# Decode attention beside a SwiGLU block on one core: one kv head of all four batches at a time, in runs of 16 to 32 KB

## The chip, the core and the metric

The kernel runs on one core of a Trainium2 chip. The metric is the device time of one execution in microseconds (us), the median of the runs shown. TensorE (PE) multiplies, VectorE (DVE), ScalarE (ACT) and GpSimd (POOL) work on elements, SyncE (SP) issues most of the transfers from the chip's memory (HBM), which 16 DMA engines carry out. A profile shows a single execution.

## The reference

One token for each of four batches goes through a layer norm, an attention over the last 4096 positions of a cache, and a SwiGLU block beside it; both are added to the input.

```python
x = A_x                                   # (4, 1, 512), bf16
xn = _layernorm(x)
# A: attention. 32 query heads, 8 kv heads, head size 128, window W = 4096 of 16384
q = (xn @ wq).reshape(4, 1, 32, 128)      # wq 512 x 4096
k = k_cache[:, :, Sk - W:, :]             # (4, 8, 4096, 128); 4 query heads share a kv head
v = v_cache[:, :, Sk - W:, :]
p = softmax(q @ k^T * 128 ** -0.5)
a = (p @ v).reshape(4, 1, 4096) @ wo      # wo 4096 x 512
# B: SwiGLU
b = (silu(xn @ w_gate) * (xn @ w_up)) @ w_down   # 512 x 1792, 512 x 1792, 1792 x 512
return x + a + b
```

The window of K is 4 x 8 x 4096 x 128 x 2 bytes, 33.55 MB, and that of V as much; the weights are 13.9 MB. Everything is read once: 81.01 MB.

## The kernel before

The attention is cut into 32 pairs of a batch and a kv head. Pair i is batch i % 4 of kv head i // 4. Its K is 1 MB, loaded as 128 partitions of 32 positions each, which makes runs of 8 KB; its V likewise. K and V have four buffers each (`KB`, `VB`, `NSL = 4`).

For each pair TensorE transposes the 32 blocks of K (128 positions x 128) in four sets of eight (`transposes`, L321), VectorE copies each set from PSUM to `KT` (`evac`, L239), TensorE multiplies each transposed block by the four query columns (`scores`, L327), ScalarE takes the exponential with no maximum subtracted (L202), and TensorE sums the probabilities with a matrix of ones (L341) and multiplies them by V (`pv`, L343). VectorE then divides (`norm`, L245 to L249). `pv` of a pair runs after the transposes of the next. Before the transposes of each pair TensorE does two matmuls of 512 columns whose result nobody reads, and before the scores a third (`spin`, L333). TensorE's part of this is a loop over the eight kv heads with the four batches written out; the other engines' instructions are written out in full.

SyncE issues nearly every load, in this order: the first half of W_Q, the input x, the second half of W_Q, K of pair 0, W_gate, W_up, W_down, V of pair 0, then K and V of the pairs in turn, then eight blocks of W_O with runs of 4 KB. A K load from the fifth on waits until the transposes of the pair four before are done (`s_tr`), a V load until the `pv` that used its buffer is done (`s_pv`).

Ahead of the loop stand the layer norm, the query projection (L295), the gate and up projections (L303), the gate on ScalarE and VectorE (L253 to L259) and the down projection (L311). Behind it the heads are reordered by matmuls with selection matrices (`permute`, L349, and `perm_copy`, L264), W_O is multiplied in four strips of 128 columns (`wo`, L357), one copy brings the result to SBUF (L279), and SyncE and ScalarE write two quarters of the output each (L191, L206).

Of the kernel before, what the change touches and what calls it, by code (L numbers as in the profile page):

```python
# [10 lines left out]
def bass_parallel_sum__sliding_block_cached__swiglu_ffn__decode_kernel(  # L11
# [18 lines left out]
    NT = W // 128  # L30
# [3 lines left out]
    NPAIR = B * HKV  # L34
    NSL = 4
    NG = 4
    SCALE = float(Dh) ** -0.5
    EPS = 1e-5

    sb = nc.alloc_sbuf_tensor  # L40
    X = sb("x_sb", [B, D], BF16)
    xc = sb("xc", [B, D], FP32)
    xsq = sb("xsq", [B, D], FP32)
    xn = sb("xn", [B, D], FP32)
    st_sum = sb("st_sum", [B, 1], FP32)
# [5 lines left out]
    WQ = sb("wq_sb", [128, NC, HQ * Dh], BF16)  # L51
    WG = sb("wg_sb", [128, NC, F], BF16)
    WU = sb("wu_sb", [128, NC, F], BF16)
    WD = sb("wd_sb", [128, NF, D], BF16)
    WO = sb("wo_sb", [128, HKV, REP, D], BF16)
    QT = sb("qT", [128, HKV, B, REP], BF16)
    QC = sb("qC", [128, B, REP], BF16)
    KB = [sb("kbuf%d" % s, [128, NT, Dh], BF16) for s in range(NSL)]
    VB = [sb("vbuf%d" % s, [128, NT, Dh], BF16) for s in range(NSL)]
    KT = [sb("kT%d" % s, [128, NT, 128], BF16) for s in range(2)]  # L60
    P = [sb("p%d" % s, [128, NT, REP], BF16) for s in range(2)]
    den = sb("den", [128, REP], FP32)
    OT = sb("oT", [128, HKV, REP, B], BF16)
    OP = sb("oP", [128, REP, HKV, B], BF16)
# [4 lines left out]
    sel = sb("sel", [128, REP, REP, 32], BF16)  # L69
    ones = sb("ones", [128, 128], BF16)  # L70
    I4 = sb("i4", [B, B], FP32)
    y0 = sb("y0", [B, D], FP32)
    I4w = sb("i4w", [B, 32], FP32)
    y = sb("y_sb", [128, 128], BF16)

    ps = nc.alloc_psum_tensor
    ps_kt = [ps("ps_kt%d" % s, [128, 512], FP32) for s in range(4)]
    ps_S = ps("ps_s", [128, 512], FP32)
    ps_O = ps("ps_o", [128, 512], FP32)
    ps_m = ps("ps_m", [128, 512], FP32)  # L80
    ps_acc = ps("ps_acc", [128, 512], FP32)

    kt_ps = [t[:].bitcast(BF16).rearrange("p (a b) -> p a b", b=128) for t in ps_kt]
    O_ps = ps_O[:, 0:REP]
    den_ps = ps_O[:, 128:128 + NT * REP]
    gate_ps = ps_m[:, 0:NF * B]
    up_ps = ps_m[:, 64:64 + NF * B]
    perm_ps = ps_m[:].rearrange("p (e k h b) -> p h e k b", e=REP, k=HKV, h=REP)
    q_ps = ps_acc[:, 0:HQ * B]
    down_ps = ps_acc[0:B, :]  # L90
    xT_ps = ps_m[:, 128:128 + NC * B]
# [4 lines left out]
    d_wq = [sem("d_wq%d" % h) for h in range(2)]  # L96
# [4 lines left out]
    d_wo = [sem("d_wo%d" % q) for q in range(HKV)]  # L101
    d_k = [sem("d_k%d" % s) for s in range(NSL)]
    d_v = [sem("d_v%d" % s) for s in range(NSL)]
# [11 lines left out]
    s_ev = sem("s_ev")  # L115
    s_sc = sem("s_sc")
    s_p = sem("s_p")
# [5 lines left out]
    s_dn = sem("s_dn")  # L123
    s_y0 = sem("s_y0")
    s_y = sem("s_y")

    x_ap = A_x.rearrange("b s d -> (b s) d")
    out_ap = out.rearrange("b s (n c) -> n (b s) c", n=NC)
# [4 lines left out]
    wo_ap = A_wo.rearrange("(k p e) n -> k p e n", k=HKV, e=REP)  # L133

    def kv_ap(cache, i):
        return cache[i % B, i // B, Sk - W:, :].rearrange("(p t) d -> p t d", t=NT)

    with nc.Block() as block:

        @block.gpsimd  # L140
        def _(eng):
            eng.memset(ident[:], 0.0)
            eng.memset(I4[:], 0.0)
            eng.memset(I4w[:], 0.0)
            eng.memset(ones[:], 1.0)
            eng.drain()
            eng.affine_select(I4[:], I4[:], pattern=[[-1, B]], compare_op=ALU.not_equal,
                              fill=1.0, base=0, channel_multiplier=1)
            eng.affine_select(ident[:], ident[:], pattern=[[-1, 128]], compare_op=ALU.not_equal,
                              fill=1.0, base=0, channel_multiplier=1)  # L150
            eng.drain()
            eng.tensor_copy(I4w[:, 0:B], I4[:])
            for e in range(REP):
                for h in range(REP):
                    eng.tensor_copy(sel[:, e, h, :], ident[:].rearrange("p (m e) -> p e m", e=REP)[:, e, :])
            eng.memset(P[1][:], 0.0)
            eng.memset(VB[NSL - 1][:], 0.0).then_inc(s_const, 1)

        @block.sync
        def _(eng):  # L160
            def load_k(i):
                if i >= NSL:
                    eng.wait_ge(s_tr, NG * (i - NSL + 1))
                eng.dma_start(KB[i % NSL][:], kv_ap(A_k_cache, i)).then_inc(d_k[i % NSL], 16)  # L164

            def load_v(i):
                if i == NSL - 1:
                    eng.wait_ge(s_pv, 1)
                if i >= NSL:
                    eng.wait_ge(s_pv, i - NSL + 2)  # L170
                eng.dma_start(VB[i % NSL][:], kv_ap(A_v_cache, i)).then_inc(d_v[i % NSL], 16)  # L171

            def load_wo(q):
                eng.dma_start(WO[:, q], wo_ap[q]).then_inc(d_wo[q], 16)  # L174

            eng.dma_start(WQ[:, 0:2], wq_ap[:, 0:2]).then_inc(d_wq[0], 16)
            eng.dma_start(X[:], x_ap).then_inc(d_x, 16)
            eng.dma_start(WQ[:, 2:4], wq_ap[:, 2:4]).then_inc(d_wq[1], 16)
            load_k(0)
# [3 lines left out]
            load_v(0)  # L183
            for i in range(1, NPAIR):
                load_k(i)
                load_v(i)
            for q in range(HKV):
                load_wo(q)
            eng.wait_ge(s_y, 1)
            for n in range(0, NC, 2):  # L190
                eng.dma_start(out_ap[n], y[32 * n:32 * n + B, :]).then_inc(d_out, 16)  # L191
            eng.wait_ge(d_out, 16 * NC)

        @block.scalar
        def _(eng):
            eng.wait_ge(s_var, 1)
# [3 lines left out]
            for j in range(NPAIR):  # L200
                eng.wait_ge(s_sc, j + 1)
                eng.activation(P[j % 2][:], ps_S[:, 0:NT * REP].rearrange("p (t h) -> p t h", h=REP),  # L202
                               ACT.Exp, scale=SCALE).then_inc(s_p, 1)
            eng.wait_ge(s_y, 1)
            for n in range(1, NC, 2):
                eng.dma_start(out_ap[n], y[32 * n:32 * n + B, :]).then_inc(d_out, 16)  # L206

        @block.vector
        def _(eng):
# [15 lines left out]
            eng.tensor_scalar(xn[:], xc[:], st_rstd[:, 0:1], None, ALU.mult).then_inc(s_xn, 1)  # L225
            eng.wait_ge(s_xT, 1)
            eng.tensor_copy(XnT[:], xT_ps.rearrange("p (c b) -> p c b", b=B)).then_inc(s_xnT, 1)
            eng.wait_ge(s_q, 1)
            eng.tensor_copy(QT[:], q_ps.rearrange("p (k h b) -> p k b h", k=HKV, b=B))
            eng.drain()  # L230
            eng.tensor_copy(QC[:], QT[:, 0]).then_inc(s_nrm, 1)

            eng.engine_nop().then_inc(s_ev, 3)

            def evac(i):
                for g in range(NG * i, NG * i + NG):
                    eng.wait_ge(s_tr, g + 1)
                    a = 8 * (g % NG)
                    eng.tensor_copy(KT[i % 2][:, a:a + 8, :], kt_ps[g % 4]).then_inc(s_ev, 1)  # L239

            def norm(j):
                eng.wait_ge(s_pv, j + 2)
                if j + B < NPAIR:
                    eng.tensor_copy(QC[:, j % B], QT[:, j // B + 1, j % B])  # L244
                eng.tensor_reduce(den[:], den_ps.rearrange("p (t h) -> p h t", h=REP), AX.X, ALU.add)  # L245
                eng.drain()
                eng.reciprocal(den[:], den[:])  # L247
                eng.drain()
                eng.tensor_tensor(OT[:, j // B, :, j % B], O_ps, den[:], ALU.mult).then_inc(s_nrm, 1)  # L249

            def ffn():
                eng.wait_ge(s_ex, 1)
                eng.tensor_scalar(ex[:], ex[:], 1.0, None, ALU.add)  # L253
                eng.drain()
                eng.reciprocal(ex[:], ex[:])
                eng.drain()
                eng.tensor_tensor(gs[:], gate_ps.rearrange("p (t b) -> p t b", b=B), ex[:], ALU.mult)
                eng.drain()
                eng.tensor_tensor(guT[:], up_ps.rearrange("p (t b) -> p t b", b=B), gs[:], ALU.mult).then_inc(s_guT, 1)  # L259

            def perm_copy(n, a, b):
                eng.wait_ge(s_pm, n)
                for h in range(REP):
                    last = eng.tensor_copy(OP[32 * h:32 * h + 32, :, a:b], perm_ps[32 * h:32 * h + 32, h, :, a:b])  # L264
                last.then_inc(s_pc, 1)

            ffn()
            for i in range(NPAIR):
# [4 lines left out]
                if i > 0:  # L273
                    norm(i - 1)
# [138 lines left out]
```

## Time and profile before

| | |
|---|---|
| median of 3 runs | 202.87 us (202.86 to 202.94) |
| span of the profiled execution | 201.0 us |
| TensorE busy | 167.7 us (83%) |
| VectorE busy | 108.7 us (54%) |
| ScalarE, GpSimd busy | 11.9 us, 7.2 us |
| main DMA queue | 81.01 MB, 97.2% of 16 engines' span |
| mean granted TensorE clock | 0.934 |

The span goes from the first to the last instruction of the profiled execution; the measured time lies 1.9 us above it. A line of a group in the profile gives the source line, the engine, the operation, output and inputs by name, shapes and count, then the busy time in us and the mean duration of one in ns, and behind the second bar the idle time of the engine ahead of it. A line of the timeline gives start and length in us. A line of a window gives its bounds, its length, the busy time and count of PE, PEld, DVE, ACT and POOL, the granted clock (PEclk), the busy share of the DMA engines and GB/s.

### The profile page before, as it was taken

Reading aid. Unit: us, or ns where it says so; the run is one execution under the profiler, and the core shown is the slowest. Engines: PE = TensorE matmul, PEld = TensorE weight load, DVE = VectorE, ACT = ScalarE, POOL = GpSimd, SP = SyncE. Lnnn points to the kernel's source line nnn. Section 1 sums busy time; section 2 is a strip of 40 time slices with the busy share of each in tenths; the row PEclk is TensorE's granted clock in tenths of the full one; section 3 lists DMA queues with packets and bytes.
Section 4 is the critical chain, followed back from the end, with each engine's and each line's share of the span. In section 5 each row is a group of like instructions: output and inputs, shape, how many; then the busy total and the mean of one; then the engine's idle time right before and its main releaser. Section 6 shows DMA issues by size and latency. Waiting matters only on the chain.

```text
span 201.0 us, 8038 instructions
## 1 busy us (share of the span) xinstructions
PE 167.7 (83%) x3635; PEld 142.7 (71%) x3635; DVE 108.7 (54%) x277; ACT 11.9 (6%) x36; POOL 7.2 (4%) x29
## 2 busy tenths in 40 slices
PE   0043778999899999999999999988898999898982
PEld 0043662788798888788877987777777987796961
DVE  0330010666666777766666666666665676565740
ACT  2020000010000000001000000000000000000000
POOL 8600000000000000000000000000000000000000
PEclk9999999999969999999999799999998899878755
DMA  6999999999999999999999999999999999999980
GB/s 232 428 425 426 431 418 414 421 417 424 422 411 419 422 422 426 422 419 419 424 422 424 422 416 421 422 424 422 422 419 421 424 424 422 421 419 412 410 334 7
DMA packets 11138, 81.15 MB, mean 404 GB/s; under 512 B 1268, under 2 KB 1272, under 8 KB 2296
## 3 DMA queue, kind: packets, MB, share of 16 engines
q1 hardware_dynamic: 11112, 81.01, 97.2%
q8 instruction: 6, 0.10, 0.2%
q14 instruction: 4, 0.03, 0.0%
q10 hardware_dynamic: 16, 0.00, 0.0%
HBM read 81.01 MB, written 0.00 MB: 403 GB/s over the span
## 4 chain that ended last, share of the span: by engine, by line
DMA 52%; PE 27%; DVE 13%; SPq 5%; issue 2%; ACT 0%; DVEq 0%
DMA kbuf<-in_A_k_cache_dram 32%; DVE kT L239 12%; DMA wu_sb<-in_B_w_up_dram 11%; PE ps_kt L321 10%; DMA wo_sb<-in_A_wo_dram 9%; PE ps_s L327 6%; SPq L174 3%; PE ps_m L333 3%; PE ps_o L343 3%; PE ps_acc L311 3%; PE ps_m L303 2%; SPq L171 1%; PE ps_o L341 0%; PE ps_acc L357 0%; SPq L164 0%
## 5 line engine op out<-in xcount | busy, mean ns | idle before, releaser
L239 DVE COPY kT<-ps_kt 128x1024 bf16<-128x1024 bf16 x128 | 80.9, 684 | 51.9 <-PE ps_kt L321 51.8
L321 PEld LDWEIGHTS ps_kt<-ident,kbuf 128*128 128x128 bf16 x1024 | 65.3, 104 | 15.1 <-issue 7.9
L321 PE MATMUL ps_kt<-ident,kbuf 128*128 128x128 bf16 x1024 | 69.4, 231 | 4.3 <-DMA kbuf<-in_A_k_cache_dram 4.2
L327 PEld LDWEIGHTS ps_s<-qC,kT 128*128 128x128 bf16 x1024 | 28.2, 96 | 12.5 <-DVE kT L239 12.0
L327 PE MATMUL ps_s<-qC,kT 128*128 128x4 bf16 x1024 | 30.4, 164 | 4.2 <-DVE kT L239 4.2
L343 PE MATMUL ps_o<-p,vbuf 128*128 128x4 bf16 x1056 | 31.5, 165 | 0.0
L343 PEld LDWEIGHTS ps_o<-p,vbuf 128*128 128x128 bf16 x1056 | 30.4, 96 | 0.8 <-issue 0.8
L333 PE MATMUL ps_m<-wq_sb,ones 128*128 128x512 bf16 x96 | 31.0, 377 | 0.0
L202 ACT ACTIVATE p<-ps_s 128x128 bf16<-128x128 f32 x32 | 8.9, 277 | 152.5 <-PE ps_s L327 152.5
L287 PE MATMUL ps_m<-i,xn 4*128 4x4 f32 x4 | 0.6, 254 | 12.3 <-DVE xn L225 12.3
L245 DVE TENSOR_REDUCE den<-ps_o 128x4 f32<-128x128 f32 x32 | 9.0, 283 | 0.6 <-PE ps_o L343 0.4
L287 PEld LDWEIGHTS ps_m<-i,xn 4*128 4x128 f32 x4 | 0.6, 208 | 12.3 <-issue 12.3
L341 PE MATMUL ps_o<-p,ones 128*128 128x128 bf16 x33 | 7.5, 228 | 0.7 <-issue 0.7
L333 PEld LDWEIGHTS ps_m<-wq_sb,ones 128*128 128x128 bf16 x96 | 7.0, 96 | 0.4 <-issue 0.4
L303 PE MATMUL ps_m<-xnT,wg_sb 128*128 128x4 bf16 x56 | 3.5, 199 | 4.4 <-DMA wg_sb<-in_B_w_gate_dram 4.4
L247 DVE RECIPROCAL den<-den 128x4 f32<-128x4 f32 x32 | 5.7, 178 | 2.7 <-issue 0.4
L249 DVE TENSOR_TENSOR oT<-ps_o,den 128x4 bf16<-128x4 f32 x32 | 5.4, 168 | 2.7 <-issue 0.4
L253 DVE TENSOR_SCALAR ex<-ex 128x56 f32<-128x56 f32 x1 | 0.2, 192 | 12.0 <-ACT ex L199 12.0
L303 PEld LDWEIGHTS ps_m<-xnT,wg_sb 128*128 128x128 bf16 x56 | 3.4, 159 | 4.5 <-DMA wg_sb<-in_B_w_gate_dram 4.5
L311 PE MATMUL ps_acc<-wd_sb,guT 128*4 128x512 bf16 x14 | 5.1, 542 | 1.7 <-DVE guT L259 1.7
L357 PE MATMUL ps_acc<-wo_sb,oP 128*4 128x128 bf16 x128 | 4.3, 305 | 1.7 <-DMA wo_sb<-in_A_wo_dram 1.7
L244 DVE COPY qC<-qT 128x4 bf16<-128x4 bf16 x28 | 4.4, 158 | 1.2 <-PE ps_o L343 1.0
(46 smaller groups left out, 41.8 us busy)
## 6 DMA issues: line engine op xcount, KB each, us to landing
kbuf<-in_A_k_cache_dram SPq DMA_DIRECT2D x32, 1024.0 KB, 15.5
vbuf<-in_A_v_cache_dram SPq DMA_DIRECT2D x32, 1024.0 KB, 13.7
wq_sb<-in_A_wq_dram SPq DMA_DIRECT2D x2, 2048.0 KB, 9.4
wo_sb<-in_A_wo_dram SPq DMA_DIRECT2D x8, 512.0 KB, 18.4
wg_sb<-in_B_w_gate_dram SPq DMA_DIRECT2D x1, 1792.0 KB, 18.5
wu_sb<-in_B_w_up_dram SPq DMA_DIRECT2D x1, 1792.0 KB, 22.3
wd_sb<-in_B_w_down_dram SPq DMA_DIRECT2D x1, 1792.0 KB, 26.1
out_dram<-y_sb SPq DMA_DIRECT2D x2, 1.0 KB
```

Source lines behind the costliest of these rows:

```text
L174: eng.dma_start(WO[:, q], wo_ap[q]).then_inc(d_wo[q], 16)
L202: eng.activation(P[j % 2][:], ps_S[:, 0:NT * REP].rearrange("p (t h) -> p t h", h=REP), ACT.Exp, scale=SCALE).then_inc(s_p, 1)
L239: eng.tensor_copy(KT[i % 2][:, a:a + 8, :], kt_ps[g % 4]).then_inc(s_ev, 1)
L245: eng.tensor_reduce(den[:], den_ps.rearrange("p (t h) -> p h t", h=REP), AX.X, ALU.add)
L247: eng.reciprocal(den[:], den[:])
L303: last = mm(o[:, t * B:(t + 1) * B], w[:].rearrange("p c (m t) -> p c t m", t=NF)[:, c, t, :], XnT[:, c, :], start=(w is WG and t == 0 and ...
L311: last = mm(down_ps, guT[:, t, :], WD[:, t, :], start=(t == 0), stop=(t == NF - 1))
L321: last = eng.transpose(kt_ps[n % 4][:, k, :], KB[b][:, 8 * g + k, :], ident[:])
L327: last = mm(ps_S[:, REP * t:REP * (t + 1)], KT[b % 2][:, t, :], QC[:, b])
L333: mm(ps_m[:], ones[:], WQ[:, 0, 0:512])
L341: mm(den_ps, ones[:], P[p % 2][:].rearrange("p t h -> p (t h)"))
L343: last = mm(O_ps, VB[p][:, t, :], P[p % 2][:, t, :], start=(t == 0), stop=(t == NT - 1))
```

## The change

The unit of work becomes a group: one kv head of all four batches. Partition p holds batch p % 4 and 128 positions, so K of a group is 4 MB in two halves of 16 KB runs, and V 4 MB in one load of 32 KB runs. K has one buffer, made of the two halves, and V one buffer.

A block of K now holds 32 positions of each of the four batches. Its transposed form is multiplied by all 16 query columns of the kv head; of the 16 scores in a row only the four of the row's own batch are meant. A new step takes the maximum of every column over its batch and adds, by one matmul per PSUM bank (`shift`), the negative maximum to the meant scores and -1e9 to the others, so that their exponential is zero. P therefore holds 16 columns per block, and `pv` sums over all four batches at once.

ScalarE takes over four of the 16 copies of transposed sets in a group (`ACT_CH`). TensorE, VectorE and ScalarE run loops over the groups; TensorE's loop has nine passes with branches, and a pass works on the K of group r and the V of group r - 1. The spins are gone. The three buffers `ps_kt` replace four.

SyncE's order of loads is new: W_Q as one load, W_gate, W_up, both halves of K of group 0, ten of the 32 rows per partition of W_O, then for each further group the two halves of its K and the V of the group before, then the last V, W_down, twenty rows and two rows of W_O. The input x is loaded by ScalarE. The down projection moves from ahead of the loop to behind it; the heads are reordered by four matmuls and one copy; W_O is multiplied in two strips of 256 columns; VectorE and ScalarE bring half of the result each to SBUF, and SyncE and ScalarE write one half each.

```diff
-    NSL = 4
-    NG = 4
+    NJ = 128 // B
+    NT = W // NJ
+    NH = B * REP
+    CH = 8
+    NCH = NT // CH
+    NB = 4
+    BT = NT // NB
+    ACT_CH = (2, 6, 10, 14)
+    WOA = 10
+    WOB = 30
...
-    KB = [sb("kbuf%d" % s, [128, NT, Dh], BF16) for s in range(NSL)]
-    VB = [sb("vbuf%d" % s, [128, NT, Dh], BF16) for s in range(NSL)]
+    KB = sb("kbuf", [128, NT, Dh], BF16, 512)
+    VB = sb("vbuf", [128, NT, Dh], BF16, 512)
...
+    def kv_ap(cache, g, a, b):
+        return cache[:, g, Sk - W:, :].rearrange("b (j t) d -> j b t d", j=NJ)[:, :, a:b, :]
...
+            def load_k(g, h):
+                if g > 0:
+                    eng.wait_ge(s_tr, NCH * (g - 1) + (h + 1) * NCH // 2)
+                eng.dma_start(KB[:, h * H:(h + 1) * H, :], kv_ap(A_k_cache, g, h * H, (h + 1) * H)).then_inc(d_k[h], 16)
+
+            def load_v(g):
+                if g > 0:
+                    eng.wait_ge(s_pv, g + 1)
+                eng.dma_start(VB[:], kv_ap(A_v_cache, g, 0, NT)).then_inc(d_v, 16)
...
+            eng.dma_start(WQ[:], wq_ap).then_inc(d_wq, 16)
+            eng.dma_start(WG[:], wg_ap).then_inc(d_wg, 16)
             eng.dma_start(WU[:], wu_ap).then_inc(d_wu, 16)
+            load_k(0, 0)
+            load_k(0, 1)
+            load_wo(0, 0, WOA)
+            for g in range(1, HKV):
+                load_k(g, 0)
+                load_k(g, 1)
+                load_v(g - 1)
+            load_v(HKV - 1)
             eng.dma_start(WD[:], wd_ap).then_inc(d_wd, 16)
+            load_wo(1, WOA, WOB)
+            load_wo(2, WOB, NR)
...
+            with eng.Fori(0, HKV) as r:
+                for n, c in enumerate(ACT_CH):
+                    eng.wait_ge(s_tr, r * NCH + (c + 1))
+                    eng.activation(KT[:, c % 4], kt_ps[c % 3], ACT.Copy).then_inc(s_ea, 1)
+                eng.wait_ge(s_pv, r + 1)
+                for q in range(NB):
+                    eng.wait_ge(s_mk, r * NB + (q + 1))
+                    eng.activation(P[:, BT * q:BT * (q + 1), :], ps_S[q][:].rearrange("p (t n) -> p t n", n=NH),
+                                   ACT.Exp, scale=SCALE).then_inc(s_p, 1)
...
+            def maxima(r):
+                eng.wait_ge(s_m, r + 1)
+                eng.transpose(mT_ps, m16[:], ident[:]).then_inc(s_mt, 1)
+
+            def shift(r):
+                eng.wait_ge(s_cm, r + 1)
+                for q in range(NB):
+                    mm(ps_S[q][:].rearrange("p (t n) -> p t n", n=NH), own[:],
+                       CM[:].unsqueeze(1).to_broadcast([NH, BT, NH]),
+                       start=False, stop=True, skip_group_check=True).then_inc(s_mk, 1)
+
+            def pv(r):
+                eng.wait_ge(d_v, r * 16)
+                for t in range(NT):
+                    last = mm(O_ps, VB[:, t, :], P[:, t, :], start=(t == 0), stop=(t == NT - 1), skip_group_check=True)
+                last.then_inc(s_pv, 1)
+
+            with eng.Fori(0, HKV + 1) as r:
+                with eng.If(r < HKV):
+                    for c in range(NCH):
+                        transposes(r, c)
+                        if c >= 2:
+                            scores(r, c - 2)
+                    scores(r, NCH - 2)
+                    scores(r, NCH - 1)
+                with eng.If(r > 0):
+                    denominators(r)
+                with eng.If(r < HKV):
+                    maxima(r)
+                with eng.If(r > 0):
+                    pv(r)
+                with eng.If(r < HKV):
+                    shift(r)
...
-            def spin(n):
-                for _ in range(n):
-                    mm(ps_m[:], ones[:], WQ[:, 0, 0:512])
...
+            for t in range(NF):
+                for n in range(2):
+                    mm(acc_ps[64 * n:64 * n + B, 0:H], guT[:, t, :], WD[:, t, H * n:H * (n + 1)],
+                       start=False, stop=False, skip_group_check=True)
+            eng.wait_ge(s_nrm, HKV + 1)
...
+            for q in range(3):
                 eng.wait_ge(d_wo[q], 16)
+                a, b = ((0, WOA), (WOA, WOB), (WOB, NR))[q]
+                for e in range(a, b):
+                    for n in range(2):
+                        last = mm(acc_ps[64 * n:64 * n + B, 0:H], OP[:, e, :], WO[:, e, H * n:H * (n + 1)],
+                                  start=False, stop=(e == NR - 1), skip_group_check=True)
```

More of the change, by code (lines that the diff above doesn't have):

```diff
@@ L50, in bass_parallel_sum__sliding_block_cached__swiglu_ffn__decode_kernel @@
     XnT = sb("xnT", [128, NC, B], BF16)
[L51 to L57, printed above, removed]
-    KB = [sb("kbuf%d" % s, [128, NT, Dh], BF16) for s in range(NSL)]
-    VB = [sb("vbuf%d" % s, [128, NT, Dh], BF16) for s in range(NSL)]
[L60 to L64, printed above, removed]
+    QT = sb("qT", [128, HKV, NH], BF16)
+    QC = sb("qC", [128, NH], BF16)
+    mx = sb("mx", [128, NB, NH], FP32)
+    m16 = sb("m16", [128, NH], BF16)
+    junk = sb("junk", [NH, 128], FP32)
+    M = sb("m", [NH, 1], FP32)
+    CM = sb("cm", [NH, NH], BF16)
+    den = sb("den", [128, NH], FP32)
+    on = sb("on", [128, NH], FP32)
+    OT = sb("oT", [128, B, HKV, REP, 4], BF16)
+    OP = sb("oP", [128, NR, B], BF16)
     ex = sb("ex", [128, NF, B], FP32)
@@ L95, in bass_parallel_sum__sliding_block_cached__swiglu_ffn__decode_kernel @@
     d_x = sem("d_x")
[L96 removed]
+    d_wq = sem("d_wq")
     d_wg = sem("d_wg")
@@ L153, in _ @@
[L153 to L157, printed above, removed]
+            eng.memset(own[:], 1.0)
+            eng.memset(moff[:], 0.0)
+            eng.memset(coff[:], 0.0)
+            eng.memset(neg[:], 0.0)
+            eng.memset(dq[:], 1.0)
+            eng.memset(dr[:], 0.0)
@@ L235, in evac @@
[L235 to L245, printed above, removed]
+            eng.reciprocal(ex[:], ex[:])
@@ L246, in norm @@
+            def norm(r):
+                eng.wait_ge(s_pv, r + 2)
+                eng.tensor_reduce(den[:], den_ps.rearrange("p (t n) -> p n t", n=NH), AX.X, ALU.add)
                 eng.drain()
@@ L309, in _ @@
+            H = D // 2
             eng.wait_ge(d_wd, 16)
+            for n in range(2):
+                mm(acc_ps[64 * n:64 * n + B, 0:H], I4[:], xf[:, H * n:H * (n + 1)],
+                   start=True, stop=False, skip_group_check=True)
             for t in range(NF):
[L311 to L322 removed]
@@ L362, in _ @@
-            eng.wait_ge(s_nrm, 1)
-            with eng.Fori(0, HKV) as r:
-                for b in range(B):
-                    spin(2)
-                    transposes(r, b)
-                    pv(r, b)
-                    spin(1)
-                    scores(r, b)
-            eng.wait_ge(s_y0, 1)
-            permute(0, HKV - 1)
-            for n in range(NC):
-                mm(ps_acc[32 * n:32 * n + 32, 0:128], I4w[:], y0[:, 128 * n:128 * n + 128],
-                   start=True, stop=False, skip_group_check=True)
```

301 lines of the change are left out of this document (155 added, 146 removed).

## The prediction, made before the changed kernel ran

> **What bounds the kernel now.** I read the page's slices first, then the rate in four windows of the trace, then the start and the end of the timeline.
>
> ```profile
> PEclk9999999999969999999999799999998899878755
> DMA  6999999999999999999999999999999999999980
> GB/s 232 428 425 426 431 418 414 421 417 424 422 411 419 422 422 426 422 419 419 424 422 424 422 416 421 422 424 422 422 419 421 424 424 422 421 419 412 410 334 7
> q1 hardware_dynamic: 11112, 81.01, 97.2%
> ```
>
> The DMA engines are full from the second slice to the 38th. The queue is the bound, and the same 81.01 MB must pass it after the change. So the change is worth what it does to three things: the rate, the moments when the queue stands empty, and what is left to do after the last landing.
>
> ```profile
> 9.00:12.00 3.00, 0.00 (x0) 0.00 (x0) 2.41 (x6) 0.74 (x2) 0.00 (x0) 1.00 1.01 431
> 40.00:170.00 130.00, 122.52 (x2730) 105.66 (x2728) 84.99 (x217) 7.77 (x28) 0.00 (x0) 0.96 1.01 421
> 188.00:194.00 6.00, 5.65 (x178) 4.98 (x180) 4.29 (x16) 0.28 (x1) 0.00 (x0) 0.78 1.02 408
> 194.00:198.00 4.00, 2.28 (x80) 1.45 (x72) 0.00 (x0) 0.00 (x0) 0.00 (x0) 0.50 0.29 114
> ```
>
> The last column is GB/s. The first three windows carry 16 KB runs (W_Q), 8 KB runs (K and V) and 4 KB runs (W_O): longer runs, higher rate. In the last window the 16 rings run dry one after the other.
>
> **The change, part by part.**
>
> *The runs.* At 421 GB/s an 8 KB packet holds one of 16 rings for 16 x 8192 B / 421 GB/s = 0.311 us; at 408 a 4 KB packet holds it for 0.161. A straight line through both gives 0.613 for 16 KB (428 GB/s; its window says 431) and 1.216 for 32 KB (431). K (33.55 MB in 16 KB runs) then takes 78.4 us instead of 79.7, V (as much, in 32 KB runs) 77.8 instead of 79.7, W_O in runs of mostly 10 and 20 KB 9.8 instead of 10.3: **3.7 us less**, and 9.80 + 9.73 = 19.5 us for a group. The ends are no gain, if the runs are cut, and about 6 us, if the longest lie above the line by as much as the first window does.
>
> *The start.* SyncE now queues W_Q, W_gate, W_up, both halves of the first group's K and ten rows of W_O. Next comes K of the second group, which must wait until the first half of group 0 is transposed, since K has one buffer.
>
> ```profile
> 25.50 3.52 PE L303 MATMUL ps_m<-xnT,wu_sb 128*128 128x4 bf16 x56 [0.78 <-DMA wu_sb<-in_B_w_up_dram]
> 30.71 5.09 PE L311 MATMUL ps_acc<-wd_sb,guT 128*4 128x512 bf16 x14 [1.69 <-DVE guT L259]
> 34.09 0.13 PEld L311 LDWEIGHTS ps_acc<-wd_sb,guT 128*4 128x4 bf16 x1 [0.30 <-issue]
> 34.51 0.78 PEld L311 LDWEIGHTS ps_acc<-wd_sb,guT 128*4 128x4 bf16 x4 [0.30 <-issue]
> L176 SPq DMA_DIRECT2D wq_sb<-in_A_wq_dram x1: 401/401/401, 0.7 to 0.7; - x1
> DMA to landing us min/median/max: 7.4/7.4/7.4
> ```
>
> W_up was waited for until 25.5. The 1.05 MB of K ahead of it (2.5 us) is gone, and W_Q's runs are longer: 22.9 now. With its 3.52 us of matmuls and 1.69 us for the gate, TensorE enters its loop at 28.1. The halves of K land at 27.8 and 32.7, the W_O rows (1.31 MB) at 35.8. A DMA into empty rings landed 7.4 us after its issue, though its 2.1 MB take 4.9: starting a dry queue costs 2.5.
>
> ```profile
> L239 DVE COPY kT<-ps_kt 128x1024 bf16<-128x1024 bf16 x128 | 80.9, 684 | 51.9 <-PE ps_kt L321 51.8
> L219 DVE TENSOR_REDUCE st_sum<-xsq 4x1 f32<-4x512 f32 x1 | 0.7, 673 | 0.1
> L245 DVE TENSOR_REDUCE den<-ps_o 128x4 f32<-128x128 f32 x32 | 9.0, 283 | 0.6 <-PE ps_o L343 0.4
> L321 PE MATMUL ps_kt<-ident,kbuf 128*128 128x128 bf16 x1024 | 69.4, 231 | 4.3 <-DMA kbuf<-in_A_k_cache_dram 4.2
> L343 PE MATMUL ps_o<-p,vbuf 128*128 128x4 bf16 x1056 | 31.5, 165 | 0.0
> L333 PE MATMUL ps_m<-wq_sb,ones 128*128 128x512 bf16 x96 | 31.0, 377 | 0.0
> L202 ACT ACTIVATE p<-ps_s 128x128 bf16<-128x128 f32 x32 | 8.9, 277 | 152.5 <-PE ps_s L327 152.5
> 99.83 1.95 PE L321 MATMUL ps_kt<-ident,kbuf 128*128 128x128 bf16 x32
> 101.67 0.95 PE L343 MATMUL ps_o<-p,vbuf 128*128 128x4 bf16 x32
> 185.11 3.42 PE L321 MATMUL ps_kt<-ident,kbuf 128*128 128x128 bf16 x32 [0.76 <-DMA kbuf<-in_A_k_cache_dram]
> ```
>
> Less one matmul's length, 32 transposes start every (1.95 - 0.23)/31 = 0.056 us at the full clock and every 0.103 at half; small matmuls every (0.95 - 0.17)/31 = 0.025. The sixteen-column scores and sums aren't in this trace: between 0.025 and a transpose's 0.056, taken at 0.025, because the weights are loaded as before and 16 columns are nearer to 4 than to 128. A block (8 transposes, 8 score matmuls) costs TensorE 0.65 us warm and 1.03 cold. Of 16 blocks VectorE copies 12 at 0.684 and takes 4 maxima over 512 values, between 0.28 and four times that; at the 0.673 of the 512-value row it needs 0.68 a block. I take 0.70 as the warm pace.
>
> The loop begins cold, as L311 did: the weight loads of L311 come 0.43 apart up to 34.5, 3.8 us after its start. With 5.1 us of half clock, the eighth block is transposed 7.0 us after the entry, at 35.1. K of group 1 is issued then and its half lands at 35.2 + 7.4 = 42.6; without the wait it would be 40.7: **1.9 lost**. Its second half waits for the sixteenth block (8 x 0.70 later, 40.7) and lands at 48.2, **0.7** behind. V of group 0 waits for nothing and lands at 57.9. From above: a cold clock for 6.8 us adds 0.6; from below: none lost, if W_up lands 2 us earlier and the clock warms at once.
>
> *The groups.* TensorE needs 16 x 0.70 plus two blocks of lead (12.6), 8 denominator matmuls of 256 columns (0.9), the sums, 128 x 0.025 + 0.2 = 3.4, and four shift matmuls of 512 columns (0.9): 17.8 of 19.5 us. The spins (96 matmuls in 31.0 us) are gone, so the clock will fall in some groups, for 3.4 us as here (PEclk is the third last column, transposes alone are counted):
>
> ```profile
> 106.29:109.70 3.41, 0.47 (x9) 0.30 (x7) 1.00 1.02 423
> 109.70:113.11 3.41, 3.10 (x31) 2.83 (x27) 0.50 1.02 423
> 113.11:116.53 3.42, 1.51 (x28) 1.61 (x29) 1.00 1.01 422
> ```
>
> A drop costs (0.103 - 0.056) x 31 = 1.5, so 19.3 at most: covered. V lands last in a group, 14.7 after the first half of K, the sums end at 18.1, and the next V has to be queued only by about 23: 5 us of lead. Under this cover lie the chain of the maximum, the doubled work on masked columns, ScalarE's four copies of 1024 values (0.28 to 2.2 us each by the 128-value row, which leaves ScalarE below 13 us) and the registers of the loops. If the cover were gone, each us above 19.5 would count eight times, less the 5. GpSimd's constants and the input row lie under W_Q's 10 us. So V of group 6 lands at 57.9 + 6 x 19.53 = 175.1.
>
> *The last V.* SyncE's order is K7, K7, V6, V7, W_down, W_O, W_O. V has one buffer, so V7 waits until V6 is multiplied. By then all K is in, and the W_down and W_O loads, whose buffers are free, stand behind that wait. V6 lands, 3.5 us of sums follow, V7 is issued at 178.7 and lands 2.5 + 9.7 later at 190.9. Without the wait: 184.8. **6.1 lost**; with sums that cost nothing it would still be 2.5.
>
> *The end.*
>
> ```profile
> 193.00 1.88 PE L357 MATMUL ps_acc<-wo_sb,oP 128*4 128x128 bf16 x64
> 197.79 0.60 PE L357 MATMUL ps_acc<-wo_sb,oP 128*4 128x128 bf16 x16 [0.74 <-DMA wo_sb<-in_A_wo_dram]
> 198.44 0.29 DVE L279 CAST y_sb<-ps_acc 128x128 bf16<-128x128 f32 x1 [4.61 <-PE ps_acc L357]
> 198.76 0.63 SPq L191 DMA_DIRECT2D out_dram<-y_sb  x2
> ```
>
> Now 0.6 us of matmuls follow the last landing. After the change W_down lands at 195.2, twenty rows of W_O at 201.3, the last two at 202.0. Four output strips ran together here (64 matmuls of 128 columns in 1.88, 0.105 for four at half clock); two strips of 256 columns then take 0.21 cold, 0.11 warm. After V7 TensorE is done with the sums at 194.4 and VectorE's normalization at 195.7. W_down's 14 pairs and the input's take 3.4 cold (198.6), reordering the heads 0.7, the first ten W_O rows 2.1 (201.4), twenty rows 4.2 cold or 2.2 warm, two rows 0.4 or 0.2. With 0.3 for the last result this is 206.3 cold, 204.1 warm; after six busy us I take 204.7. So **2.7 us** of matmuls follow the last landing, and the copy and the output DMA take 2.4 (198.4 to 201.0 was 2.6, with two DMAs on each queue). The span is 207.1. The measured 202.87 stands 1.9 above this execution's span of 201.0: **209.0**.
>
> **The rivals.**
>
> *TensorE stays cold without the spins.* The Trainium skill (TensorE: Matmul & The Clock Gate, Part 4: PE-mode transpose) says that transposes do not count as work for the clock gate. By that rule most of the loop's work would not count. The window above speaks against it: 3.10 of its 3.41 us were transposes, and the clock was back at 1.00 in the next. If it happened: 18 x 1.03 + 1.8 + 3.6 + 1.8 = 25.7 a group, 8 x 6.2 - 5 more, 254 us. Chance 0.03.
>
> *The four batches collide in memory.* Four runs of one DMA now lie 33.55 MB apart instead of 8 KB. Rings that move together read different tokens of one batch, as before, so I expect nothing; no row here shows such a distance. At half the rate K and V would take 156 us more, 365. The Trainium skill (DMA: Bandwidth & Descriptors, the row on HBM row pitch at large powers of two) tells of copies that fall to half at pitches of megabytes; no run here shows it. Chance 0.03.
>
> *TensorE's groups are longer than 19.5.* If a sixteen-column matmul costs a transpose's 0.056, the scores and sums add 256 x 0.031 = 7.9, so 25.7 a group, 254 again; if only half of that, 21.8, and 8 x 2.3 - 5 = 13 more: 222. Chance 0.07.
>
> *The long runs are cut.* Then 3.7 is not gained: 212.7. Chance 0.05.
>
> *Not slower.* The losses stand as summed, but the long runs go further above the line. It decides from 6.1 us: K and V in 150.1 instead of 156.2, 447 GB/s; 202.9. For it, the rate rises at each step of 408, 421, 431; against it, by ever less per doubled run. Chance 0.08.
>
> **How the numbers follow.** My forecast, 209.0, has 0.74. Its range: from below, no loss at the start (2.6) and a warm end (0.6) with 2.0 from long runs that lie above the line, 203.8; from above, no gain of runs (3.7) and a cold end (1.6), 214.3. That leaves out part of the last rival and the three slow cases, less than 2 in 10. Faster than 202.87 by over 0.2% (0.4 us, about what this measurement can tell): most of the last rival, 0.06; within it 0.02; slower 0.92.
>
> **What would show it right or wrong.** Right: K and V windows near 428 to 431 GB/s; two dips in the slices, one near 36 us and one of about 6 us near 176; V7's wait for the sums among the queue's waits; W_O matmuls for some 3 us after the last landing; PEclk falling in most groups while DMA stays full. Wrong: TensorE never waiting for K or V in the middle, a flat GB/s row, or a rate of 440 and more.

## The result, and the profile after

The changed kernel takes 208.6 us (median of 4 runs, 208.08 to 210.42), the kernel before 202.89 beside it: a ratio of 1.0295, interval 1.0251 to 1.0339. Five more runs later gave 208.88 and 1.0298 (1.0281 to 1.0315). The forecast was 209.0. The profiled execution has a span of 206.4 and a time of 208.08.

The slices of the changed kernel's page, 5.16 us each, its main queue, its queue of instructions, and the engines' shares of the chain that ended last:

```profile
PEclk9999999966996699699759975997999599855569
DMA  7989995999999999999999999999999995289991
GB/s 249 464 371 428 433 420 238 356 403 454 411 441 457 394 413 416 486 413 413 416 486 413 413 422 480 413 416 429 470 391 435 451 451 248 51 381 426 438 393 43
q1 hardware_dynamic: 4472, 81.01, 92.4%
q8 instruction: 6, 0.10, 0.2%
...
PE 63%; DMA 25%; DVE 5%; ACT 4%; issue 2%; SPq 1%; DVEq 0%
```

The same bytes now take 92.4% of the span in place of 97.2%. The DMA row has two holes, slice 7 (the rate is still low in slice 8) and slices 34 and 35. The windows of the trace measure them:

```profile
34.00:36.40 2.40, 2.40 (x65) 2.40 (x62) 2.39 (x5) 1.02 (x1) 0.00 (x0) 1.00 0.07 24
60.00:172.00 112.00, 109.75 (x2334) 98.89 (x2333) 74.50 (x147) 35.92 (x47) 0.00 (x0) 0.85 1.01 432
172.00:176.00 4.00, 3.63 (x77) 2.94 (x75) 3.08 (x7) 1.02 (x1) 0.00 (x0) 1.00 0.36 156
176.00:180.00 4.00, 3.98 (x117) 3.03 (x113) 1.19 (x5) 0.81 (x2) 0.00 (x0) 0.94 0.00 0
```

Between the holes the queue is faster than before, 432 GB/s against 421: for the 67.1 MB of K and V 155.3 us in place of 159.4. Then from about 174 to 180 almost nothing moves, while TensorE works nearly without a pause on what it has. Who makes the queue wait stands in the waits of SyncE's queue (us in total, times, longest), and who waits for V in those of TensorE:

```profile
SPq L210 <- PE ps_kt L370: 111.3, 14, 30.4
SPq L215 <- PE ps_o L410: 51.3, 7, 19.1
```

```profile
PE ps_o L410 <- DMA vbuf<-in_A_v_cache_dram: 8.3, 2, 8.1
```

Most of SyncE's waiting is harmless, since earlier loads are still under way. It costs only where nothing is left in the rings: at K of group 1, and at V7. TensorE waits for V twice in eight groups, and 8.1 of the 8.3 us are V7. The timeline of the end:

```profile
175.45 3.39 PE L410 MATMUL ps_o<-p,vbuf 128*128 128x16 bf16 x128
178.87 0.54 SPq L215 DMA_DIRECT2D vbuf<-in_A_v_cache_dram  x1
191.28 3.58 PE L410 MATMUL ps_o<-p,vbuf 128*128 128x16 bf16 x128 [8.08 <-DMA vbuf<-in_A_v_cache_dram]
194.90 0.42 DVE L316 TENSOR_REDUCE den<-ps_o 128x16 f32<-128x256 f32 x1 [14.62 <-PE ps_o L410]
195.52 1.02 PE L433 MATMUL ps_kt<-xf,i 4*4 4x256 f32 x4 [0.66 <-DMA wd_sb<-in_B_w_down_dram]
196.47 3.15 PE L437 MATMUL ps_kt<-wd_sb,guT 128*4 128x256 bf16 x28
200.38 3.77 PE L449 MATMUL ps_kt<-wo_sb,oP 128*4 128x256 bf16 x64 [0.53 <-DVE oP L332]
201.58 2.27 PEld L449 LDWEIGHTS ps_kt<-wo_sb,oP 128*4 128x4 bf16 x44 [0.24 <-DMA wo_sb<-in_A_wo_dram]
204.19 0.41 DVE L334 CAST y_sb<-ps_kt 4x256 bf16<-4x256 f32 x1 [3.87 <-PE ps_kt L449]
```

V7 is issued the moment V6's sums are done and lands 12.4 us later. From the end of V7's sums to the copy of y another 9.3 us pass (194.90 to 204.19), in which TensorE waits 0.66 us for W_down and its weight loads (PEld) 0.24 us for W_O.

### The profile page after: what moved, and what is told of

It reads as the page before. It is cut to its first block, busy times and chain, and to the rows that moved or that the text cites. A ratio compares the mean times of both kernels' runs of the same rounds, so it can differ in the third digit from the quotient of the medians.

```text
span 206.4 us, 7990 instructions
## 1 busy us (share of the span) xinstructions
PE 169.8 (82%) x3520; PEld 150.4 (73%) x3520; DVE 109.2 (53%) x217; ACT 52.6 (25%) x69; POOL 7.5 (4%) x29
## 3 DMA queue, kind: packets, MB, share of 16 engines
q1 hardware_dynamic: 4472, 81.01, 92.4%
## 4 chain that ended last, share of the span: by engine, by line
PE 63%; DMA 25%; DVE 5%; ACT 4%; issue 2%; SPq 1%; DVEq 0%
PE ps_kt L370 30%; PE ps_o L410 12%; DMA wu_sb<-in_B_w_up_dram 10%; PE ps_s L383 10%; DMA wd_sb<-in_B_w_down_dram 8%; DMA vbuf<-in_A_v_cache_dram 7%; PE ps_s L403 5%; ACT kT L248 4%; DVE mx L304 2%; PE ps_kt L449 2%; PE ps_s L356 2%; PE ps_kt L437 1%; DVE m L306 1%; PE ps_kt L398 1%; PE ps_kt L433 0%
## 5 line engine op out<-in xcount | busy, mean ns | idle before, releaser
L370 PE MATMUL ps_kt<-ident,kbuf 128*128 128x128 bf16 x1024 | 89.3, 243 | 2.1 <-DVE guT L290 2.1
L299 DVE COPY kT<-ps_kt 128x1024 bf16<-128x1024 bf16 x96 | 64.4, 691 | 21.4 <-PE ps_kt L370 21.2
L248 ACT ACTIVATE kT<-ps_kt 128x1024 bf16<-128x1024 bf16 x32 | 32.7, 1023 | 58.8 <-PE ps_kt L370 58.8
L383 PE MATMUL ps_s<-qC,kT 128*128 128x16 bf16 x1024 | 45.2, 171 | 2.3 <-ACT kT L248 2.3
L383 PEld LDWEIGHTS ps_s<-qC,kT 128*128 128x128 bf16 x1024 | 39.6, 98 | 3.4 <-ACT kT L248 3.0
L410 PE MATMUL ps_o<-p,vbuf 128*128 128x16 bf16 x1024 | 27.4, 170 | 8.3 <-DMA vbuf<-in_A_v_cache_dram 8.3
L252 ACT ACTIVATE p<-ps_s 128x512 bf16<-128x512 f32 x32 | 16.5, 603 | 46.6 <-PE ps_s L403 46.6
L304 DVE TENSOR_REDUCE mx<-ps_s 128x16 f32<-128x512 f32 x32 | 21.9, 683 | 3.6 <-PE ps_s L383 3.6
L403 PE MATMUL ps_s<-cm,own 16*128 16x512 bf16 x32 | 12.7, 536 | 2.2 <-issue 2.2
L393 PE MATMUL ps_o<-p,ones 128*128 128x256 bf16 x64 | 9.1, 290 | 1.4 <-ACT p L252 1.3
```

Of the source, the lines that this page charges most:

```text
L248: eng.activation(KT[:, c % 4], kt_ps[c % 3], ACT.Copy).then_inc(s_ea, 1)
L252: eng.activation(P[:, BT * q:BT * (q + 1), :], ps_S[q][:].rearrange("p (t n) -> p t n", n=NH), ACT.Exp, scale=SCALE).then_inc(s_p, 1)
L299: eng.tensor_copy(KT[:, c % 4], kt_ps[c % 3]).then_inc(s_ev, 1)
L304: eng.tensor_reduce(mx[:, q, :], ps_S[q][:].rearrange("p (t n) -> p n t", n=NH), AX.X, ALU.max)
L370: last = eng.transpose(kt_ps[c % 3][:, k, :], KB[:, CH * c + k, :], ident[:])
L383: last = mm(ps_S[q][:, NH * t:NH * (t + 1)], KT[:, c % 4, k, :], QC[:], start=(t == 0), stop=False, skip_group_check=True)
```

## The experiments

### The last V without its wait

W_Q's buffer has the size of one V and is free after the query projection. V7 goes there, waits only for that, and TensorE's last pass is written out behind the loop.

```diff
-            load_v(HKV - 1)
+            eng.wait_ge(s_q, 1)
+            eng.dma_start(WQF, kv_ap(A_v_cache, HKV - 1, 0, NT)).then_inc(d_v7, 16)
```

> V of the last group goes into W_Q's place, which is free after the query projection, and waits for nothing but that; the last pass of TensorE's loop is written out behind the loop. All else is the changed kernel (span 206.4, 208.6 us). By the sum of the prediction the queue loses 6.1 us on that wait: V7 should land near 185 instead of 191.2, everything behind it 6.1 earlier, span 200.3, time 202.5. Rival: TensorE's own passes set the end, because it is behind the queue (its chain runs from 45 to 141 us without a DMA in it); then V7 lands early, the sums of the last group still start only when TensorE is through, and less than 3 us are gained: 205.6 or more.

Measured: 202.46 us (12 runs, 201.53 to 205.41), ratio to before 0.9972 (0.9954 to 0.9991). Its windows, and its end:

```profile
33.70:36.50 2.80, 2.80 (x68) 2.80 (x67) 2.42 (x5) 1.02 (x1) 0.00 (x0) 1.00 0.09 31
172.00:176.00 4.00, 3.54 (x72) 3.04 (x69) 3.35 (x6) 1.02 (x1) 0.00 (x0) 1.00 0.99 426
176.00:180.00 4.00, 4.00 (x132) 3.61 (x133) 1.20 (x4) 0.16 (x1) 0.00 (x0) 1.00 0.93 401
```

```profile
189.15 0.42 DVE L319 TENSOR_REDUCE den<-ps_o 128x16 f32<-128x256 f32 x1 [8.21 <-PE ps_o L414]
198.64 0.41 DVE L337 CAST y_sb<-ps_kt 4x256 bf16<-4x256 f32 x1 [4.11 <-PE ps_kt L455]
```

Where 156 and 0 GB/s stood, 426 and 401 stand; the first hole is still there. 208.6 - 202.46 is 6.1 us, the price that the prediction put on this wait; in the two profiled executions the copy of y comes 5.6 us earlier (198.64 against 204.19), so the agreement to a tenth is chance. The rival, a gain of less than 3 us, is out. This one wait is the whole difference between slower and not slower.

### K of group 1 without its wait

The same buffer, given to K of group 1 in place of V7; the first two passes and the last are written out.

```diff
+                if g == 1:
+                    if h == 0:
+                        eng.wait_ge(s_q, 1)
+                    eng.dma_start(WQF[:, h * H:(h + 1) * H, :],
+                                  kv_ap(A_k_cache, g, h * H, (h + 1) * H)).then_inc(d_k1[h], 16)
+                    return
```

> K of the second group goes into W_Q's place and waits only for the query projection; the first two passes and the last are written out. The stop of the queue near 36 us should be gone from the slices. By the sum of the prediction that stop costs 1.9 + 0.7 = 2.6 us: time 206.0. Rival: TensorE reaches its second pass only at 46.8 us, 4 us after the first half of K has landed, and stays late through the next passes; then no more than about 1 us is gained: 207.6 or more.

Measured: 212.05 us (6 runs), ratio 1.0468 (1.0434 to 1.0502). Both theories missed: the rival's "207.6 or more" holds as a number only, for it spoke of a small gain and 3.4 us were lost. Windows of its trace, and its queue of instructions:

```profile
34.00:38.00 4.00, 4.00 (x102) 4.00 (x100) 3.99 (x7) 2.05 (x2) 0.00 (x0) 1.00 0.97 416
63.50:66.50 3.00, 2.74 (x46) 1.60 (x46) 1.08 (x4) 0.90 (x2) 0.00 (x0) 0.57 0.50 142
```

```profile
q8 instruction: 12, 0.20, 0.3%
```

```profile
63.76 1.27 PE L423 MATMUL ps_o<-p,vbuf 128*128 128x16 bf16 x42 [0.97 <-issue]
65.06 0.54 SPq L223 DMA_DIRECT2D vbuf<-in_A_v_cache_dram  x1
82.89 1.81 PE L423 MATMUL ps_o<-p,vbuf 128*128 128x16 bf16 x65 [0.33 <-issue]
177.17 3.42 PE L423 MATMUL ps_o<-p,vbuf 128*128 128x16 bf16 x128 [0.28 <-DMA vbuf<-in_A_v_cache_dram]
```

The hole at 34 us is gone and a new one stands at 63.5 to 66.5: V of group 1 waits for V0's sums, which end at 65.0, K of group 2 is in by then, and all other loads stand behind that wait. The loads had run ahead of TensorE, which enters its loop only at 28 us, and the hole has moved to the next wait. The written-out passes added a cost of their own: twice the instruction packets (12; 6 in the changed kernel), and gaps of 0.97 and 0.33 us inside runs of sums in which TensorE waited for nothing that the profile shows. V6's sums begin 1.7 us later than in the changed kernel (177.17 against 175.45). Of the 3.4 us in the medians the rest came behind V7, where the first matmuls of W_O's twenty rows started at 204.79 in place of 201.58; what caused that part isn't settled.

### Runs of 8 KB

K in four loads and V in four, so that every run is 8 KB, as before the change.

```diff
-                eng.dma_start(VB[:], kv_ap(A_v_cache, g, 0, NT)).then_inc(d_v, 16)
+                for a in range(0, NT, 32):
+                    eng.dma_start(VB[:, a:a + 32, :], kv_ap(A_v_cache, g, a, a + 32)).then_inc(d_v, 16)
```

> The same order and the same buffers, but each half of K goes in two loads and V in four, so that runs are 8 KB as in the kernel before. If the queue sets the pace of the groups (19.4 us with long runs at 432 GB/s), a group takes 19.9 at 421 GB/s, and the time rises by 8 x 0.47 = 3.5 us less what a stop hides: 211 to 212. If TensorE's pass (18.8 to 19.1 us) sets it, the time rises by less than 1.5: below 210.

Measured: 210.87 us (7 runs), ratio 1.0396 (1.0383 to 1.0410), 2.3 us above the changed kernel, between the two expectations. The window of the middle:

```profile
60.00:172.00 112.00, 109.93 (x2332) 99.14 (x2332) 74.41 (x146) 35.95 (x47) 0.00 (x0) 0.83 1.01 427
```

427 GB/s against 432, for 67.1 MB of K and V, is 67,100 x (1/427 - 1/432) us, 1.8 us. So the length of the runs is worth about 2 us and no more. The number of issues changed with it (four for a V take SyncE 2.48 us, one took 0.54), and no run separates the two. The rest of the step from 421 to 432 came with something else in the new order or layout, which no run separates.

### Is the middle bound by the queue or by a cold TensorE?

PEclk falls in the middle of the changed kernel, as the prediction had it; but TensorE waits for almost nothing there, where the prediction had it waiting for loads. To keep the clock up, one matmul of 240 columns, into columns nobody reads, after every ten sums:

```diff
+                    if t % 10 == 9:
+                        mm(ps_O[:, 16:256], ones[:], WQ[:, 0, 0:240], start=False, stop=False, skip_group_check=True)
```

> The changed kernel with a matmul of 240 columns into unused columns of the sums' bank after every ten sum matmuls: twelve more in each pass, some 1.2 us of TensorE at full clock, in the stretch of a pass that streams the fewest columns. Its output is unchanged. Theory (in the middle the queue and TensorE go at nearly the same pace, 19.4 us for a group by the landings and 18.8 to 19.1 us of TensorE for a pass): with more columns in the windows of the sums the granted clock no longer drops to half there; a pass then costs TensorE 17.8 + 1.2 - 0 = 19.0 us or less, the landings of a group stay at 19.4 us, and the time stays at 208.6, between 207.4 and 209.6. Rival (the two half-clock windows of each pass are what the kernel waits for): without the drops a pass goes at the rate of the bytes alone, 19.0 us or less for each group, and the time falls by 2 us or more, to 206.6 or less.

Measured: 213.72 us (6 runs, 212.78 to 217.36), ratio 1.0543 (1.0512 to 1.0575). Both missed. The middle's window, TensorE's wait for V, and five lines of the timeline:

```profile
60.00:172.00 112.00, 106.89 (x2417) 96.57 (x2414) 74.62 (x148) 35.92 (x47) 0.00 (x0) 0.97 1.00 426
```

```profile
PE ps_o L410 <- DMA vbuf<-in_A_v_cache_dram: 9.9, 4, 7.8
```

```profile
176.15 0.41 PE L410 MATMUL ps_o<-p,vbuf 128*128 128x16 bf16 x10 [0.91 <-DMA vbuf<-in_A_v_cache_dram]
...
181.50 0.42 DVE L316 TENSOR_REDUCE den<-ps_o 128x16 f32<-128x256 f32 x1 [5.30 <-PE ps_o L410]
193.87 0.43 PE L410 MATMUL ps_o<-p,vbuf 128*128 128x16 bf16 x10 [7.83 <-DMA vbuf<-in_A_v_cache_dram]
...
199.89 0.42 DVE L316 TENSOR_REDUCE den<-ps_o 128x16 f32<-128x256 f32 x1 [16.98 <-PE ps_o L410]
208.80 0.41 DVE L334 CAST y_sb<-ps_kt 4x256 bf16<-4x256 f32 x1 [4.22 <-PE ps_kt L451]
```

The part of the theory about the middle held: the granted clock there rose from 0.85 to 0.97, TensorE now waited for V four times in place of twice, and V6's sums began at 176.15 against 175.45, no earlier. The added matmuls cost TensorE time themselves, so this alone doesn't give the price of the drops. The changed kernel's own trace does: V6, queued at 159.26, landed 15.9 us later at 175.15, 0.3 us before its sums began. With the queue full up to there, a faster TensorE had 0.3 us to gain; the queue hid the rest. What the expectation left out are the passes that nothing hides. V6's sums, on which V7's issue hangs, took 5.3 us from 176.15 to 181.5 in place of 3.4, part of that at half clock, so V7 was issued 2.6 us later. V7's sums ended at 199.89 in place of 194.90, and y came 4.6 us later. The same twelve matmuls are free in most of the middle and cost 1.9 us in V6's sums and 2.4 us in V7's (193.87 to 199.89 in place of 191.28 to 194.90). They aren't free in V0's sums either: V of group 1 is queued at 65.74 in place of 63.92, the queue moves 291 GB/s in place of 442 between 66 and 70 us, and most of the step from 432 to 426 in the window above lies there; from 70 to 100 us both kernels move 427 to 428.

### What makes the last 9.3 us

Three kernels: 20 rows of W_O in place of 10 loaded early (`WOA = 20`); the down projection and W_O in four strips of 128 columns; both.

```diff
-                    for n in range(2):
-                        last = mm(acc_ps[64 * n:64 * n + B, 0:H], OP[:, e, :], WO[:, e, H * n:H * (n + 1)],
+                    for n in range(4):
+                        last = mm(acc_ps[32 * n:32 * n + B, 0:H], OP[:, e, :], WO[:, e, H * n:H * (n + 1)],
```

> 20 instead of 10 of W_O's 32 rows are loaded ahead of K of the second group, so 1.3 MB (3.1 us) less follow the last V. If the last landing sets the end, as the prediction's list of landings has it (W_O last at 202.2), the span falls by up to 3 us: 203.4, time 205.6. If the end is TensorE's work behind the last V (64 W_O matmuls in one run of 3.8 us from 200.4 on, after the down projection), the landings come 3 us earlier and the time stays within 1 us of 208.6.

> The changed kernel with the down projection and the output projection in four strips of 128 columns in place of two of 256 (twice as many matmuls of half the width, four on different columns of the array), one copy and four small output transfers. Its output is unchanged. Theory (TensorE's work behind V7 sets the end: sums, denominators, down projection 3.15 us, W_O 3.77 us, with 0.24 us of waiting for W_O): the two go from 6.9 us to 3.5 to 5 us, the wait for the last of W_O grows by what is gained until the landing at 202.2 is reached, so the end comes 1.5 to 2.5 us earlier, less some 0.3 us for the two further output transfers: 206.1 to 207.4. Rival (the last landing sets it, as the prediction had it): 2.7 us of matmuls behind it shrink by 1 us at most and the four outputs take it back: 207.8 or more.

> The changed kernel with four strips at its end and with 20 rows of W_O in place of 10 loaded after K of group 0, so that 12 rows are left for the end of the queue. Its output is unchanged. In the changed kernel, with the 20 rows alone and with the strips alone, the stretch from the end of V7's sums to the copy of y took 9.3 us each time. Theory (two bounds of the same length lie side by side there, TensorE's 9.3 us of work, and the landing of W_O with the matmuls behind it, so that shortening either changes nothing): with both shortened the 2.1 us in which the strips waited for W_O are gone, the stretch takes 7.0 to 7.6 us, and the time is 1.5 to 2.5 us under the changed kernel beside it. Rival (something else fixes the 9.3 us): within 0.7 us of it.

> The changed kernel as it is, beside the one above on the same chip: 208.1 to 209.2 us by its first four runs, whose median was 208.6.

Measured: 20 rows 208.62 us (5 runs), ratio 1.0278 (1.0265 to 1.0291); strips 209.22 (6 runs), 1.0306 (1.0271 to 1.0340); both 206.97 (5 runs), 1.0186 (1.0158 to 1.0213), beside the changed kernel again at 208.88, 1.0298 (1.0281 to 1.0315). Each alone changes nothing beyond the scatter, both together 1.9 us. First the end of the 20 rows alone in its timeline, then W_O with the strips alone, then the end of both:

```profile
196.30 0.42 DVE L316 TENSOR_REDUCE den<-ps_o 128x16 f32<-128x256 f32 x1 [14.58 <-PE ps_o L410]
201.87 3.66 PE L449 MATMUL ps_kt<-wo_sb,oP 128*4 128x256 bf16 x64 [0.53 <-DVE oP L332]
205.57 0.41 DVE L334 CAST y_sb<-ps_kt 4x256 bf16<-4x256 f32 x1 [3.75 <-PE ps_kt L449]
```

```profile
198.95 1.24 PE L452 MATMUL ps_kt<-wo_sb,oP 128*4 128x128 bf16 x40 [0.53 <-DVE oP L335]
201.98 2.52 PE L452 MATMUL ps_kt<-wo_sb,oP 128*4 128x128 bf16 x88 [1.79 <-DMA wo_sb<-in_A_wo_dram]
```

```profile
195.93 0.42 DVE L319 TENSOR_REDUCE den<-ps_o 128x16 f32<-128x256 f32 x1 [14.78 <-PE ps_o L413]
199.53 3.42 PE L452 MATMUL ps_kt<-wo_sb,oP 128*4 128x128 bf16 x128 [0.53 <-DVE oP L335]
203.01 0.29 DVE L337 CAST y_sb<-ps_kt 128x128 bf16<-128x128 f32 x1 [3.53 <-PE ps_kt L452]
```

With the 20 rows W_O is in before TensorE asks for it, and the stretch still takes 9.3 us (196.30 to 205.57). TensorE waits in it 0.77 us for W_down and 0.53 for VectorE's copy; the rest is its own work. With the strips TensorE is ready for W_O earlier and then stands 1.79 us before the landing; with both the run of W_O isn't broken, and the stretch takes 7.1 us (195.93 to 203.01). That is 2.2 us less, of which the end keeps 1.2 in this execution (203.01 against 204.19): V7's sums end 1.0 us later (1.4 with the 20 rows alone), which fits the rows that now stand ahead of every V in the queue. So two bounds lay side by side here: TensorE's own work with those two waits, and the landing with the matmuls behind it. The expectation for the strips had called the first the only one.

### The stops covered and the end shortened

V7 in W_Q's buffer; W_down and four rows of W_O loaded right behind K of group 0; the down projection ahead of the last sums; four strips; the rest of W_O in three loads.

```diff
-            load_wo(0, 0, WOA)
+            eng.dma_start(WD[:], wd_ap).then_inc(d_wd, 16)
+            load_wo(0, 0, WO_CUT[1])
...
+            for n in range(4):
+                mm(acc_ps[32 * n:32 * n + 32, 0:H], I4w[:], xf[:, H * n:H * (n + 1)],
...
+            denominators(HKV)
+            pv(HKV)
```

> The kernel with V7 in W_Q's place (202.46 us), with four strips at the end as above, W_down and four rows of W_O loaded right behind K of group 0 (so that they cover the queue's stop there), the down projection ahead of the last denominators and sums, and the rest of W_O in three loads. Its output is unchanged. Theory (the two stops of the queue and TensorE's tail are the whole loss): W_down's 4.2 us of queue leave the end of the queue and fall partly into the first stop of 2.6 us, so V7 lands between 185 and 187.5 and the last of W_O between 193.5 and 196; behind it some 1 to 2 us of matmuls, the copy and the output transfer of 2 us: span 197 to 199, time 198.5 to 201, under both kernels. Rival (the queue's first stop only moves, as it did with K of group 1 in that place): 201.5 to 202.5.

Measured: 199.34 us (5 runs, 199.15 to 199.95), ratio to before 0.9819 (0.9806 to 0.9831): faster than both kernels. Its slices of 4.95 us and its end:

```profile
DMA  6999999999999999999999999999999999999980
GB/s 219 437 424 424 444 424 426 368 348 444 452 394 424 454 437 394 431 460 431 404 434 447 431 414 431 460 431 411 431 470 431 397 427 454 437 431 431 402 373 20
q1 hardware_dynamic: 4624, 81.01, 96.5%
```

```profile
189.63 0.42 DVE L321 TENSOR_REDUCE den<-ps_o 128x16 f32<-128x256 f32 x1 [8.20 <-PE ps_o L416]
195.42 0.29 DVE L339 CAST y_sb<-ps_kt 128x128 bf16<-128x128 f32 x1 [3.66 <-PE ps_kt L457]
```

No slice falls under nine tenths between the first and the last two. Slices 8 and 9, at 368 and 348, are what is left of the first hole. From the last sums to the copy it takes 5.8 us, against 9.5 in the kernel that moved V7 alone, whose last sums ended 0.5 us earlier; that difference, 3.2, is the gain over it, 3.1.

## Why the prediction was right

It held in sign, in size and in most of its steps. That it also met the time to 0.4 us is in part luck, as said below the table.

| step | forecast | measured |
|---|---|---|
| TensorE enters the loop | 28.1 | 28.45 |
| first hole, K of group 1 queued | 35.1 | 35.08 |
| landings of its halves | 42.6, 48.2 | 42.7, 49.0 |
| V of group 0 lands | 57.9 | 58.6 |
| a group's landings | 19.53 | 19.42 |
| V6 lands | 175.1 | 175.15 |
| V7 queued, landed | 178.7, 190.9 | 178.87, 191.2 |
| last W_O landing | 202.0 | 202.2 |
| last matmul of TensorE | 204.7 | 204.15 |
| span, time | 207.1, 209.0 | 206.4, 208.6 (this execution 208.08) |

Several steps agree because two misses cancel. TensorE entered the loop 0.35 us late and then needed 6.6 us for eight blocks in place of 7.0. V of group 0 landed 0.7 us late, and six groups of 19.42 in place of 19.53 made up 0.7, so that V6 landed on time. At the end 0.7 us less of matmuls stands against landings that came 0.2 to 0.4 us late.

**V7's wait**, 6.1 us, is shown: with it gone the kernel gained 6.1 us by the medians and 5.6 in the profiled executions. The queue lost it from about 174 to 180.

**The first hole**, 1.9 and 0.7 us, is there at its place but is longer. The early W_O rows landed at 35.6, the halves of K of group 1 7.1 and 6.3 us after what stood before them, though each half's bytes take 4.9: 2.2 and 1.4 us, 3.6 in place of 2.6. What it was worth was also read too simply. Taking the wait away doesn't return it: it reappears at V of group 1. In these runs only bytes that wait for nothing returned part of it: the 20 rows loaded early put 3.1 us of bytes more ahead, and V6 landed 1.4 us later; in the last kernel slices 8 and 9 are what is left.

**The runs**: the rate forecast, 428 to 431, came out at 432, but the reason given carries only about half of it. With 8 KB runs the new kernel still moves 427.

**The groups**: covered, as forecast, yet more narrowly than the sum said. From V0's sums (60.48) to V6's (175.45) a pass took 19.16 us on the mean, against 17.8 without a drop of the clock and 19.3 with one, which the sum called the most. Here its sizes were wrong: the clock was at half for 6.8 us, two windows of 3.4, in four of the six passes, which took 19.4 to 19.7 us, and for one window in the other two, which took 18.3 and 18.4. A drop cost about 1.2 us, not 1.5, and there were more of them. TensorE holds 63% of the chain of waits. That "TensorE never waiting for K or V in the middle" would show it wrong was thus too strong a test: between 46 and 172 us it waited for V once, 0.3 us, and its weight loads three times for K, 2.1 us. The two paces lie little over 1% apart, and V6 landed, from a queue that was full all along (share 1.01 from 60 to 172 us), only 0.3 us before its sums: TensorE's pace can't have cost more than that.

**The sizes taken between bounds** came out well: sixteen-column matmuls start every 0.025 us (128 sums in 3.39 us), ScalarE's copy of 1024 values takes 1.02 us, VectorE's maximum over 512 values 0.683 against the 0.673 taken:

```profile
L248 ACT ACTIVATE kT<-ps_kt 128x1024 bf16<-128x1024 bf16 x32 | 32.7, 1023 | 58.8 <-PE ps_kt L370 58.8
L304 DVE TENSOR_REDUCE mx<-ps_s 128x16 f32<-128x512 f32 x32 | 21.9, 683 | 3.6 <-PE ps_s L383 3.6
```

**The end**: 2.7 us of matmuls after the last landing were forecast, 2.0 came. The term hid that TensorE's own work behind V7 took just as long, so a gain on either side alone would have been forecast wrongly.

**The rivals**: the cold TensorE (granted clock 0.85 in the middle, with the spins gone), the collision of four batches (432 GB/s) and the long groups did not occur. The long runs were not cut: the same bytes went in 4472 packets in place of 11112. The rate stayed far from the 447 from which the change would not have been slower.

## What to carry to other kernels

With one buffer each, a loop's first and last load are where a full queue runs dry; price each wait by what is still in the rings when it ends, and give the last one a dead buffer. A hole shrinks when bytes that wait for nothing stand ahead of it; here, making one load earlier moved it to the next wait. When a cut at the end brings nothing, look for a second bound of the same length before calling the first one wrong, and remember that work free in a covered pass is paid in full where the cover has not begun or has ended.

## What the runs showed of the hardware that was not expected

- A higher granted clock bought no time: 0.97 against 0.85 in the middle (60 to 172 us), with V6's sums beginning 0.7 us later, not earlier. At 0.85 TensorE was only 0.3 us behind V6's landing; more than that the low PEclk can't have cost up to there.
- At the loop's entry the PEclk row reads 1.00 (28.45 to 32.40 us), yet the first 24 transposes take 2.74 us, some 0.11 us each, about the 0.103 that the prediction read at half clock. The row doesn't show the pace there.
- Loads whose four parts lie 33.55 MB apart showed no loss: 432 GB/s, against 421 before. The Trainium skill (DMA: Bandwidth & Descriptors, the row on HBM row pitch at large powers of two) tells of copies that halve at pitches of 4 MiB and 8 MiB; nothing like it appears in this trace.
- Runs of the same 8 KB moved at 421 GB/s in the kernel before and at 427 in the changed order; the cause is open.
- Writing passes out in place of looping doubled the instruction packets, and TensorE stood for up to 0.97 us in the middle of a run of matmuls that waited for nothing shown. That the fetches caused the gaps is argued from one run that has more of both, not shown.
